# Attention's scores and products with v as 64x64 tiles, two row halves side by side, on one Trainium2 core

## The chip, the cores and the metric

The kernel runs on one core of one Trainium2 chip, in one launch. The metric is the device time of that launch in microseconds (us). A core has five engines that run their own instruction streams in order and wait for each other by semaphores: TensorE (PE, with its weight loads shown as PEld), VectorE (DVE), ScalarE (ACT), GpSimd (POOL) and SyncE (SP, which here only issues DMAs).

## The reference, cut to what matters

```
B, H, S, D = 8, 8, 576, 64; chunks of 64 tokens
scores = q_c @ k_c.T / 8                       (64x64 per batch, head and chunk)
attn   = exp(scores - max) / (sum + 1e-9)
x      = attn @ v_c  -> 4608 tokens x 512
logits = x @ w_gate                            (8 experts, 576 tokens each, by rank)
y[tokens of e] = relu(x @ w1[e]) @ w2[e]       (512 -> 1024 -> 512)
out = maximum(y @ m1, y @ m2, y @ m3) @ m_out  (512 -> 768 -> 512)
```

Everything is float32. The change touches only the first three lines of it.

## The kernel before, in words

The program has three stages: attention with the router's logits (the function `attention`), the experts, and the last layer with three weights. Only the first one changes; the second can't begin before all logits are there, so the first one's end moves what follows.

Attention works on 36 groups of 128 tokens (two chunks of 64) with all eight heads. Four groups are a unit; there are nine units, and q, k and v are loaded by units (`load_qk`, `load_v`), q and k into two buffers, v into three. One group goes through a pipeline of steps, and one pass of the loop at the end of the function (`for i in range(G + 2)`) issues one step of several groups:

- `scores(i)`: per pair of heads and per chunk one matmul. Its stationary operand is q's transpose for one chunk, [128 rows, 64 columns]: 64 rows of an even head and, under them, 64 rows of an odd head. Its moving operand is a block of `KB`, [128 rows, 128 columns], whose upper half has k's transpose of the even head in the first 64 columns and zeros in the others, and whose lower half has zeros first and then the odd head. So one matmul gives both heads' scores side by side, and half of the products are by zero.
- `trans` and `evac`: for the next unit, k and q are transposed on PE into PSUM (four transposes each) and copied to SBUF in two halves, r = 0 and 1. k's first half is copied by ACT, its second by DVE; both of q's by ACT. DVE's half of one tile waits for ACT's half.
- `smax(i)`, `ssub(i)` on DVE: maximum and subtraction, from PSUM. `expo(i)` on ACT: the exponential. `sums(i - 1)` on DVE: sum, plus 1e-9, reciprocal.
- `att_t(i - 1)`, `att_c(i - 1)`: the weights transposed on PE, copied to `AT` by ACT; `pv(i - 1)`: the product with v, again with 128 moving columns of which half are zero blocks (`VB`), into PSUM tile `pX`, which has one buffer.
- `scale(i - 2)` on DVE: `pX` times the reciprocal, and a store of x to DRAM by POOL; `x_t`, `x_c`: x transposed on PE, copied by ACT; `logit1`, `logit2`: once in four groups the gate's logits.

The zero blocks are written once, by memsets: four on DVE (first k and v buffers) and six on POOL. The order on each engine is the order in which the loop issues: there is no scheduler (`tc.manual_schedule()`). PSUM has eight banks, and all are in use: `pT` 2, `pS` 2, `pA`, `pX`, `pY`, `pL` one each.

Of the kernel before, what the change touches and what calls it, by code (L numbers as in the profile page):

```python
# [7 lines left out]
F32 = mybir.dt.float32  # L8
# [20 lines left out]
def attention(ctx, tc, q, k, v, wg_in, xd, L, ident, early, mark):  # L29
# [57 lines left out]
    def trans(nm, u, n):  # L87

        mark(nm + "T")
        if nm == "q" and n == 0:  # L90
            QT[u] = P.tile([128, 4, 8, 64], F32, name="qT")
        pt = PS.tile([128, 2, 2, 128], F32, name="pT")
        PT[nm, u, n] = pt
        for a in range(2):
            for w in range(2):
                h = 4 * (n // 2) + 2 * a + n % 2
                nc.tensor.transpose(pt[:, a, w, :], QK[nm, u][:, h, w * 128:w * 128 + 128], ident)  # L97

    def evac(nm, u, n, r, eng):
        mark(nm + "E")  # L100
        s, h0 = n % 2, 2 * (n // 2)
        src = PT[nm, u, n][r * 64:r * 64 + 64].rearrange("p a w t -> p a t w")
        o = slice(s * 64, s * 64 + 64)
        if nm == "q":
            dst = QT[u][o, h0:h0 + 2].rearrange("p a j (i w r) -> p a (j i) w r", w=2, r=2)[:, :, :, :, r]
        else:
            dst = KB[u % 2][o, :, h0:h0 + 2, s].rearrange("p j a (i w r) -> p a j i w r", w=2, r=2)[:, :, :, :, :, r]
            src = src.rearrange("p a (j i) w -> p a j i w", j=8)
        (nc.vector.tensor_copy if eng else nc.scalar.copy)(dst, src)

    def scores(g):
        mark("scores")
        u, h = divmod(g, 4)
        ps = PS.tile([128, 4, 128], F32, name="pS")
        PSS[g] = ps
        for hp in range(4):
            for c in range(2):
                nc.tensor.matmul(ps[c * 64:(c + 1) * 64, hp, :], QT[u][:, hp, 2 * h + c, :],  # L118
                                 KB[u % 2][:, 2 * h + c, hp].rearrange("p s i -> p (s i)"),
                                 start=True, stop=True)  # L120

    def smax(g):
        mark("soft")
        MX[g] = P.tile([128, 8], F32, name="mx")
        nc.vector.tensor_reduce(MX[g], PSS[g].rearrange("p a (s i) -> p (a s) i", s=2), op=OP.max, axis=AX.X)

    def ssub(g):
        mark("soft")
        A[g] = P.tile([128, 8, 64], F32, name="A0")
        nc.vector.tensor_tensor(A[g], PSS[g].rearrange("p a (s i) -> p (a s) i", s=2),  # L130
                                MX[g][:, :, None].to_broadcast([128, 8, 64]), op=OP.subtract)

    def expo(g):
# [28 lines left out]
    def pv(g):  # L162
        mark("pv")
        u, h = divmod(g, 4)
        PX[g] = PS.tile([128, 4, 128], F32, name="pX", bufs=1)
        for hp in range(4):
            for c in range(2):
                nc.tensor.matmul(PX[g][c * 64:(c + 1) * 64, hp, :], AT[g][:, hp, c * 64:c * 64 + 64],  # L168
                                 VB[u % 3][:, 2 * h + c, hp].rearrange("p s i -> p (s i)"),
                                 start=True, stop=True)  # L170

    def scale(g):
        mark("scale")
        X[g] = P.tile([128, 8, 64], F32, name="x", bufs=3)
        nc.vector.tensor_tensor(X[g], PX[g].rearrange("p a (s i) -> p (a s) i", s=2),
                                R[g][:, :, None].to_broadcast([128, 8, 64]), op=OP.mult)
        nc.gpsimd.dma_start(xd[g * 128:(g + 1) * 128, :], X[g].rearrange("p h d -> p (h d)"))

# [24 lines left out]
    def logit2(j, w0=0, w1=4):  # L203
        mark("logit2")
        pl = PS.tile([128, 4, 4, 32], F32, name="pL", bufs=1) if w0 < 3 else PS.tile([128, 4, 4, 32], F32, name="pS")
        for w in range(w0, w1):
            nc.tensor.transpose(pl[:, w].rearrange("p a e -> p (a e)"), LS[j][:, w * 128:(w + 1) * 128], ident)
        nc.vector.tensor_reduce(L[:, 4 * j + w0:4 * j + w1, :],
                                pl[:, w0:w1, :, :8].rearrange("p w a e -> p w e a"), op=OP.add, axis=AX.X)

    for n in range(4):
# [5 lines left out]
    def on(j):  # L217
        return 0 <= j < G

    for i in range(G + 2):  # L220
        u, n = i // 4 + 1, i % 4
        tr = u < NU
        if tr:
            load_v(u, n)
        if u + 1 < NU:
            load_qk(u + 1, n // 2, "kq"[n % 2])
        if on(i):
            scores(i)
        if tr:
            trans("k", u, n)  # L230
        if on(i - 1):
            att_t(i - 1)
        if tr:
            trans("q", u, n)
        if on(i - 2):
            scale(i - 2)
            if i == G + 1:
                logit1(8, 0, 3)
            x_t(i - 2)
        if on(i):  # L240
            smax(i)
        if on(i - 1):
            sums(i - 1, 0)
        if on(i):
            ssub(i)
        if on(i - 1):
            sums(i - 1, 1)
        if tr:
            evac("k", u, n, 0, 0)
        if on(i - 1):  # L250
            att_c(i - 1)
            pv(i - 1)
        if tr:
            evac("k", u, n, 1, 1)
            evac("q", u, n, 0, 0)
        if on(i):
            expo(i)
        if on(i - 1):
            sums(i - 1, 2)
        if tr:  # L260
            evac("q", u, n, 1, 0)
        if i >= 6 and (i - 3) % 4 == 3 and i < G:
            logit1((i - 3) // 4)
        if i >= 7 and (i - 4) % 4 == 3 and i < G:
            logit2((i - 4) // 4)
        if on(i - 2):
            x_c(i - 2)
        if i == G + 1:
# [932 lines left out]
```

## Time and profile before

| | before |
|---|---|
| median of 3 runs | 1247.35 us (1246.78 to 1247.45) |
| profiled execution, its own time | 1249.4 us |
| its span | 1247.6 us |
| PE busy in the span | 1190.3 us (95%), 8909 matmul records |
| DVE busy | 835.6 us (67%) |
| ACT busy | 431.9 us (35%) |
| mean granted TensorE clock | 0.982 |
| attention | from the start to about 182 us of the span |

The page of the profile shows one execution: busy time of each engine, the span in 40 slices, the DMA queues, the chain of waits that ended last, and groups of instructions by source line. The trace behind it gives every instruction's start and length, in windows or in order of time. A float32 matmul shows as two records (two passes), a transpose as one.

### The profile page before, as it was taken

The page shows a single profiled execution, that of the slowest core. Times are in us where ns is not written, and L with a number is a line of the kernel's source. Part 1 is how long each engine was busy: PE and PEld are TensorE (multiplying, and loading weights), DVE is VectorE, ACT ScalarE, POOL GpSimd, SP SyncE. Part 2 cuts the span into 40 slices and gives each one's busy share as a digit, 9 for nine tenths or more (in the row PEclk, how much of TensorE's full clock was granted, in tenths as well). Part 3 has the DMA queues.
Part 4 walks back from the last instruction along what each step waited for, and adds up shares of the span by engine and source line. Part 5 has one row for each costly group of instructions (what it writes and reads, how often), then busy time and mean ns, then how long its engine had stood idle before and what let it go on. Part 6 is the DMA issues. An engine that isn't in the chain of part 4 may idle for free.

```text
span 1247.6 us, 22277 instructions
## 1 busy us (share of the span) xinstructions
PE 1190.3 (95%) x8909; PEld 1109.0 (89%) x8909; DVE 835.6 (67%) x1686; ACT 431.9 (35%) x691; POOL 242.6 (19%) x365
## 2 busy tenths in 40 slices
PE   5999978999999999997999999999999999999996
PEld 4888854899999999997999998998998998998995
DVE  6888876887797988796824466566565565665660
ACT  3888842333334343434423122213113113113111
POOL 7222211010235344444420001001001002002001
PEclk9999996999999999999999999999999999999998
DMA  9999713364647565757653474564663663763641
GB/s 212 255 242 259 197 60 115 123 203 137 203 138 235 173 229 169 236 164 239 220 199 138 185 265 177 222 255 164 250 256 136 261 253 128 287 259 110 237 153 51
DMA packets 148778, 243.05 MB, mean 195 GB/s; under 512 B 39490, under 2 KB 111938, under 8 KB 141762
## 3 DMA queue, kind: packets, MB, share of 16 engines
q1 hardware_dynamic: 129234, 184.05, 46.2%
q0 software_dynamic: 14016, 47.98, 11.2%
q10 hardware_dynamic: 5424, 9.59, 2.1%
q8 instruction: 70, 1.15, 0.4%
q14 instruction: 34, 0.28, 0.1%
HBM read 195.12 MB, written 46.47 MB: 194 GB/s over the span
## 4 chain that ended last, share of the span: by engine, by line
PE 40%; issue 36%; DVE 13%; POOL 4%; DMA 4%; ACT 2%; POOLq 0%; SPq 0%; DVEq 0%; ACTq 0%
PE acc L1014 10%; PE acc L972 9%; PE pX L168 3%; PE pT L97 3%; PE pS L118 2%; POOL out_dram L1137 2%; PE py L1053 2%; DVE chunk L702 2%; PE po L1129 2%; DVE hlo L992 2%; DMA xg<-xd,idx 2%; PE px L1053 2%; PE pz L1053 2%; DMA inq<-in_q_dram 1%; PE pA L155 1%
## 5 line engine op out<-in xcount | busy, mean ns | idle before, releaser
L972 PE MATMUL acc<-xhi,chunk 128*128 128x288 f32 x1024 | 208.7, 303 | 8.0 <-DVE hlo L992 7.3
L1014 PE MATMUL acc<-hhi,chunk 128*128 128x288 f32 x1024 | 211.3, 300 | 2.8 <-DVE hlo L992 2.8
L972 PEld LDWEIGHTS acc<-xhi,chunk 128*128 128x128 f32 x1024 | 162.4, 190 | 9.6 <-DVE hlo L992 8.2
L1014 PEld LDWEIGHTS acc<-hhi,chunk 128*128 128x128 f32 x1024 | 162.7, 188 | 4.1 <-DVE hlo L992 3.7
L1014 PE MATMUL acc<-hlo,chunk 128*128 128x288 f32 x512 | 151.2, 295 | 1.4 <-DVE hlo L992 1.2
L1129 PE MATMUL po<-chunk,h 128*128 128x512 f32 x648 | 149.3, 390 | 0.0
L1137 POOL DMA_INDIRECT out_dram<-ot,ia x36 | 35.7, 990 | 560.6 <-ACT ot L1135 560.6
L972 PE MATMUL acc<-xlo,chunk 128*128 128x288 f32 x512 | 144.2, 297 | 0.0
L1129 PEld LDWEIGHTS po<-chunk,h 128*128 128x128 f32 x648 | 121.5, 188 | 24.8
L1053 PE MATMUL px<-xb,wa 128*128 128x384 f32 x648 | 130.0, 334 | 0.7 <-ACT ys L1021 0.7
L1053 PE MATMUL py<-xt,wb 128*128 128x384 f32 x648 | 129.8, 334 | 0.0
L1053 PEld LDWEIGHTS px<-xb,wa 128*128 128x128 f32 x648 | 114.0, 188 | 1.3 <-ACT ys L1021 1.0
L1053 PEld LDWEIGHTS py<-xt,wb 128*128 128x128 f32 x648 | 114.0, 188 | 0.5
L1074 ACT CAST h<-best 128x384 fp32r<-128x384 f32 x72 | 37.0, 513 | 198.2 <-DVE best L1072 121.3
L1014 PEld LDWEIGHTS acc<-hlo,chunk 128*128 128x128 f32 x512 | 96.0, 188 | 2.3 <-DVE hlo L992 2.3
L972 PEld LDWEIGHTS acc<-xlo,chunk 128*128 128x128 f32 x512 | 94.6, 190 | 0.0
L702 DVE TENSOR_TENSOR chunk<-raw,chunk 128x1024 fp32r<-128x1024 f32 x67 | 81.7, 1224 | 13.2 <-ACT chunk L695 13.2
L984 ACT ACTIVATE hhi<-acc 128x576 fp32r<-128x576 f32 x64 | 41.6, 650 | 110.7 <-PE acc L972 94.2
L1089 ACT COPY tmp<-px 128x384 f32<-128x384 f32 x54 | 25.8, 477 | 146.3 <-PE px L1053 146.3
L992 DVE SCALAR_TENSOR_TENSOR hlo<-acc,hhi 128x576 fp32r<-128x576 f32 x64 | 48.1, 753 | 40.5 <-ACT hhi L984 40.4
L695 ACT CAST chunk<-raw 128x1024 fp32r<-128x1024 f32 x67 | 69.7, 1047 | 9.9 <-ACT ys L1021 6.4
L732 POOL DMA_INDIRECT xg<-xd,idx x40 | 42.5, 1062 | 146.2 <-DVE ohe L622 74.9
(211 smaller groups left out, 2036.5 us busy)
## 6 DMA issues: line engine op xcount, KB each, us to landing
wb<-wdb SPq DMA_DIRECT2D x54, 1024.0 KB
wa<-wda SPq DMA_DIRECT2D x54, 768.0 KB
raw<-in_moe_w_dram SPq DMA_DIRECT2D x64, 512.0 KB
xd<-x POOLq DMA_DIRECT2D x36, 256.0 KB
yd<-ys ACTq DMA_DIRECT2D x32, 288.0 KB
wdb<-pair POOLq DMA_DIRECT2D x18, 512.0 KB
yraw<-yd SPq DMA_DIRECT2D x12, 768.0 KB
vb<-in_v_dram SPq DMA_DIRECT2D x112, 64.0 KB
```

Source lines behind the costliest of these rows:

```text
L97: nc.tensor.transpose(pt[:, a, w, :], QK[nm, u][:, h, w * 128:w * 128 + 128], ident)
L168: nc.tensor.matmul(PX[g][c * 64:(c + 1) * 64, hp, :], AT[g][:, hp, c * 64:c * 64 + 64], VB[u % 3][:, 2 * h + c, hp].rearrange("p s i -> p ...
L695: nc.scalar.copy(hi, raw)
L702: nc.vector.tensor_tensor(lo, raw, hi.bitcast(F32), op=OP.subtract)
L732: nc.gpsimd.indirect_dma_start(out=g, out_offset=None, in_=xd[:, :], in_offset=bass.IndirectOffsetOnAxis(ap=rt.idx[r][:, t:t + 1], axis=0))
L972: nc.tensor.matmul(acc[:, hf, :288], w[a][:, dc, o:o + 128], x[:, dc, tk], start=n == 0, stop=n == 11)
L984: nc.scalar.activation(hv, acc[:, :, :288], AF.Relu)
L992: nc.vector.scalar_tensor_tensor(hl[:, f].rearrange("p (a t) -> p a t", a=2), acc[:, :, :288], 0.0, hv.bitcast(F32), op0=OP.max, op1=OP.su ...
L1014: nc.tensor.matmul(acc[:, hf, :288], w[a][:, f, :], x[:, f, tk], start=n == 0, stop=n == 23)
L1053: nc.tensor.matmul(dst, w[:, dc, o, a], XO[x][:, c, dc], start=start and n == 0, stop=stop and n == 5, skip_group_check=True)
L1129: nc.tensor.matmul(PO[t], h[:, x, t % 6 * 128:t % 6 * 128 + 128], w[a][:, f % 2], start=f == 0 and n == 0, stop=f == 5 and n == 2)
L1137: st = nc.gpsimd.indirect_dma_start(out=out, out_offset=bass.IndirectOffsetOnAxis(ap=ia[:, t:t + 1], axis=0), in_=ot, in_offset=None)
```

## The change

- The zero blocks go: `VB` has [128, 8, 4, 64], k's transposes go into a tile `kT` of the same form as `qT`, and the ten memsets are gone.
- One matmul is now [64 rows, 64 columns] by 64 moving columns. There are 16 for a group's scores and 16 for its product with v, in place of 8 and 8. They are issued together by `half(g, f, e)`: in the first half the scores of group g for even heads (rows 0 to 63 of the array) beside the product of group e for odd heads (rows 64 to 127), two of the one and two of the other in turn; then `nc.tensor.drain()`; then the second half with rows swapped. Scores and product write different PSUM tiles.
- The product with v is one loop pass later: `half(i, 0, i - 2)`, and x's transposes two passes after the weights' (`x_t(i - 3)`). The loop has one pass more (G + 3).
- The order inside a pass is written anew: k's copies right behind k's transposes, `scale` ahead of `smax`, `ssub` right behind `smax`, all three steps of `sums` at the end, both of q's copies ahead of `expo`, and `x_c` last.
- x has four buffers in place of three.

```diff
                 (nc.gpsimd if u and j % 2 and s else nc.sync).dma_start(
-                    t[s * 64:(s + 1) * 64, j, :, s, :],
+                    t[s * 64:(s + 1) * 64, j],
...
-    VB = [C.tile([128, 8, 4, 2, 64], F32, name="vb%d" % i) for i in range(3)]
-    KB = [C.tile([128, 8, 4, 2, 64], F32, name="kb%d" % i) for i in range(2)]
-    for t, eng in ((KB[0], nc.vector), (VB[0], nc.vector), (KB[1], nc.gpsimd), (VB[1], nc.gpsimd),
-                   (VB[2], nc.gpsimd)):
-        eng.memset(t[0:64, :, :, 1, :], 0.0)
-        eng.memset(t[64:128, :, :, 0, :], 0.0)
+    VB = [C.tile([128, 8, 4, 64], F32, name="vb%d" % i) for i in range(3)]
...
-    def scores(g):
...
-                nc.tensor.matmul(ps[c * 64:(c + 1) * 64, hp, :], QT[u][:, hp, 2 * h + c, :],
-                                 KB[u % 2][:, 2 * h + c, hp].rearrange("p s i -> p (s i)"),
-                                 start=True, stop=True)
+    def half(g, f, e):
+
         for hp in range(4):
+            for x, s in ((g, f), (e, 1 - f)):
+                for c in range(2):
+                    o, to = slice(s * 64, s * 64 + 64), slice(c * 64, c * 64 + 64)
+                    if x == g and on(g):
+                        mark("scores")
+                        u, h = divmod(g, 4)
+                        out, a, b = PSS[g], QT["q", u][o, hp, 2 * h + c], QT["k", u][o, hp, 2 * h + c]
+                    elif x == e and on(e):
+                        mark("pv")
+                        u, h = divmod(e, 4)
+                        out, a, b = PX[e], AT[e][o, hp, to], VB[u % 3][o, 2 * h + c, hp]
+                    else:
+                        continue
+                    nc.tensor.matmul(out[to, hp, s], a, b, start=True, stop=True, tile_position=(s * 64, c * 64))
...
-    for i in range(G + 2):
+    for i in range(G + 3):
...
+        if i == G + 2:
+            logit1(8, 0, 3)
+        if on(i) or on(i - 2):
+            half(i, 0, i - 2)
+            nc.tensor.drain()
+            half(i, 1, i - 2)
         if tr:
             trans("k", u, n)
+            for r in range(2):
+                evac("k", u, n, r, r)
         if on(i - 1):
             att_t(i - 1)
-        if tr:
-            trans("q", u, n)
         if on(i - 2):
             scale(i - 2)
-            if i == G + 1:
-                logit1(8, 0, 3)
-            x_t(i - 2)
         if on(i):
             smax(i)
         if on(i - 1):
-            sums(i - 1, 0)
+            att_c(i - 1)
+        if tr:
+            trans("q", u, n)
+            for r in range(2):
+                evac("q", u, n, r, 0)
         if on(i):
             ssub(i)
...
+        if on(i - 3):
+            x_t(i - 3)
...
+            for st in range(3):
+                sums(i - 1, st)
         if on(i):
             expo(i)
...
+        if on(i - 3):
+            x_c(i - 3)
```

How the instructions stand now is shown at two places. The first is ACT in one pass in the middle of attention (`kb` or `kT`: k's half; `AT`: the transposed weights; `qT`: q's halves; `A`: the exponential; `xT`: x's transpose). Before:

```order
L109 COPY kb_178<-pT 64x2x8x32 [waits PE_49]
L160 COPY AT<-pA 128x512 [waits PE_49,Activation_49]
L109 COPY qT<-pT 64x512 [waits PE_49]
L136 ACTIVATE A<-A_1162 128x512 [waits DVE_49,Activation_49]
L109 COPY qT<-pT 64x512
L191 COPY xT<-pY 128x4x128 [waits PE_49]
```

Now:

```order
L99 COPY kT<-pT 64x512 [waits PE_49]
L157 COPY AT<-pA 128x512 [waits PE_49,Activation_49]
L99 COPY qT<-pT 64x512 [waits PE_49]
L99 COPY qT<-pT 64x512
L133 ACTIVATE A<-A_1370 128x512 [waits DVE_49,Activation_49]
L178 COPY xT<-pY 128x4x128 [waits PE_49]
```

The second copy of q has moved ahead of the exponential, which has one copy (x's) between itself and the next pass's copy of k. The second place is DVE in the same pass (`x`: the scaling, `mx` and the `A` behind it: maximum and subtraction, `sm` and `rc`: sums and reciprocal). Before:

```order
L175 TENSOR_TENSOR x<-pX,rc 128x512 [waits DMASW7_49,DVE_49,PE_49]
L125 TENSOR_REDUCE mx<-pS 128x8 [waits PE_49]
L143 TENSOR_REDUCE sm<-A 128x8 [waits Activation_49]
L130 TENSOR_TENSOR A_1300<-pS,mx 128x512 [waits DVE_49]
L145 TENSOR_SCALAR sm<-sm 128x8 [waits DVE_49]
L109 COPY kb_178<-pT 64x2x8x32 [waits Activation_49]
L148 RECIPROCAL rc<-sm 128x8 [waits DVE_49]
```

Now:

```order
L99 COPY kT<-pT 64x512 [waits Activation_49]
L162 TENSOR_TENSOR x<-pX,rc 128x512 [waits DMASW1_49,DVE_49]
L122 TENSOR_REDUCE mx<-pS 128x8
L127 TENSOR_TENSOR A_1716<-pS,mx 128x512 [waits DVE_49]
L140 TENSOR_REDUCE sm<-A 128x8
L142 TENSOR_SCALAR sm<-sm 128x8 [waits DVE_49]
L145 RECIPROCAL rc<-sm 128x8 [waits DVE_49]
```

k's copy, which waits for ACT, has moved from behind the subtraction to the head of the pass.

## Rows read from the trace of the kernel before

**Rows 1.** Windows of 10 us: busy time and records of each engine, granted clock, DMA.

```profile
core 0: us, PE busy (x) PEld busy (x) DVE busy (x) ACT busy (x) POOL busy (x), PEclk, DMA share, GB/s
...
90.00:100.00 10.00, 9.98 (x125) 9.06 (x125) 9.05 (x18) 8.35 (x16) 3.39 (x6) 1.00 1.11 242
...
130.00:140.00 10.00, 9.97 (x116) 8.21 (x115) 8.07 (x17) 8.29 (x15) 3.38 (x6) 1.00 1.15 300
...
190.00:200.00 10.00, 7.25 (x59) 3.44 (x59) 6.33 (x30) 0.00 (x0) 0.00 (x0) 0.50 0.01 2
```

**Rows 2.** Timeline of one pass, PE: start us, us, engine, line, operation, tiles.

```profile
108.39 0.66 PE L97 MATMUL pT<-ident,ink 128*128 128x128 f32 x4
...
110.29 1.11 PE L168 MATMUL pX<-vb,AT 128*64 128x128 f32 x16
...
111.21 1.06 PE L118 MATMUL pS<-kb,qT 128*64 128x128 f32 x16
...
112.20 0.66 PE L97 MATMUL pT<-ident,ink 128*128 128x128 f32 x4
```

**Rows 3.** Timeline: k's transposes of passes 3 and 31, and the stage's end.

```profile
33.96 0.33 PE L97 MATMUL pT<-ident,ink 128*128 128x128 f32 x1
...
155.98 0.66 PE L97 MATMUL pT<-ident,ink 128*128 128x128 f32 x4
...
181.98 1.20 PE L411 MATMUL rp<-ident,mm 128*128 128x128 f32 x4 [0.92 <-DVE t L392]
```

**Rows 4.** Timeline, ACT and DVE in the same passes; in brackets idle time before.

```profile
109.08 0.63 ACT L109 COPY kb<-pT 64x512 f32<-64x512 f32 x1 [0.89 <-PE pT L97]
...
109.60 0.59 ACT L160 COPY AT<-pA 128x512 f32<-128x512 f32 x1
...
110.07 0.64 ACT L109 COPY qT<-pT 64x512 f32<-64x512 f32 x1
...
110.58 0.64 ACT L136 ACTIVATE A<-A 128x512 f32<-128x512 f32 x1
...
111.24 0.64 ACT L109 COPY qT<-pT 64x512 f32<-64x512 f32 x1
...
114.30 0.70 DVE L109 COPY kb<-pT 64x512 f32<-64x512 f32 x1
...
115.03 0.20 DVE L148 RECIPROCAL rc<-sm 128x8 f32<-128x8 f32 x1
...
115.68 0.69 DVE L175 TENSOR_TENSOR x<-pX,rc 128x512 f32<-128x512 f32 x1 [0.45 <-PE pX L168]
...
116.29 0.68 DVE L125 TENSOR_REDUCE mx<-pS 128x8 f32<-128x512 f32 x1
```

**Rows 5.** Timeline of the start: k's two copies, ACT's half and DVE's half.

```profile
12.14 0.63 ACT L109 COPY kb<-pT 64x512 f32<-64x512 f32 x1 [4.84 <-PE pT L97]
...
12.80 0.69 DVE L109 COPY kb<-pT 64x512 f32<-64x512 f32 x1 [2.69 <-ACT kb L109]
```

**Rows 6.** Timeline of the last passes, without transposes of q and k.

```profile
161.98 0.68 DVE L130 TENSOR_TENSOR A<-pS,mx 128x512 f32<-128x512 f32 x1
...
162.76 0.63 ACT L136 ACTIVATE A<-A 128x512 f32<-128x512 f32 x1 [0.76 <-DVE sm L145]
...
165.33 0.68 DVE L130 TENSOR_TENSOR A<-pS,mx 128x512 f32<-128x512 f32 x1
```

**Rows 7.** The router's product, 32-column tiles: ns min/median/max, first and last start us, forms.

```profile
L600 PE MATMUL rp<-aoh x288: 179/215/249, 204.9 to 571.3; 128*32 128x40 bf16 x144
```

**Rows 8.** Timeline: one burst of that line on PE.

```profile
204.86 0.75 PE L600 MATMUL rp<-aoh 128*32 128x40 bf16 x36 [0.33 <-DVE aoh L578]
```

**Rows 9.** Timeline of the start: DVE's last memset and PE's first weight load.

```profile
8.35 1.76 DVE L79 MEMSET vb<- 64x2048 f32 x1 [0.47 <-issue]
...
10.99 0.71 PEld L97 LDWEIGHTS pT<-ident,ink 128*128 128x128 f32 x4 [10.99 <-DVE vb L79]
```

**Rows 10.** Waits of SP's queue up to 180 us: us in total, times, longest.

```profile
SPq L53 <- DMA ident<-unit: 3.8, 1, 3.8
```

More of the change, by code (lines that the diff above doesn't have):

```diff
@@ L89, in trans @@
         mark(nm + "T")
-        if nm == "q" and n == 0:
-            QT[u] = P.tile([128, 4, 8, 64], F32, name="qT")
+        if n == 0:
+            QT[nm, u] = P.tile([128, 4, 8, 64], F32, name=nm + "T")
         pt = PS.tile([128, 2, 2, 128], F32, name="pT")
@@ L102, in evac @@
         src = PT[nm, u, n][r * 64:r * 64 + 64].rearrange("p a w t -> p a t w")
[L103 to L108, printed above, removed]
-        (nc.vector.tensor_copy if eng else nc.scalar.copy)(dst, src)
-    def scores(g):
[L112 to L115, printed above, removed]
-        for hp in range(4):
-            for c in range(2):
-                nc.tensor.matmul(ps[c * 64:(c + 1) * 64, hp, :], QT[u][:, hp, 2 * h + c, :],
-                                 KB[u % 2][:, 2 * h + c, hp].rearrange("p s i -> p (s i)"),
-                                 start=True, stop=True)
+        dst = QT[nm, u][s * 64:s * 64 + 64, h0:h0 + 2].rearrange("p a j (i w r) -> p a (j i) w r", w=2, r=2)[:, :, :, :, r]
+        (nc.vector.tensor_copy if eng else nc.scalar.copy)(dst, src)
+    def half(g, f, e):
+        for hp in range(4):
+            for x, s in ((g, f), (e, 1 - f)):
[12 more added lines that the diff above has]
+                    nc.tensor.matmul(out[to, hp, s], a, b, start=True, stop=True, tile_position=(s * 64, c * 64))
     def smax(g):
@@ L124, in smax @@
         MX[g] = P.tile([128, 8], F32, name="mx")
-        nc.vector.tensor_reduce(MX[g], PSS[g].rearrange("p a (s i) -> p (a s) i", s=2), op=OP.max, axis=AX.X)
+        nc.vector.tensor_reduce(MX[g], PSS[g].rearrange("p a s i -> p (a s) i"), op=OP.max, axis=AX.X)
     def ssub(g):
@@ L160, in att_c @@
         nc.scalar.copy(AT[g], PA[g])
[L162 to L170, printed above, removed]
     def scale(g):
         mark("scale")
-        X[g] = P.tile([128, 8, 64], F32, name="x", bufs=3)
-        nc.vector.tensor_tensor(X[g], PX[g].rearrange("p a (s i) -> p (a s) i", s=2),
+        X[g] = P.tile([128, 8, 64], F32, name="x", bufs=4)
+        nc.vector.tensor_tensor(X[g], PX[g].rearrange("p a s i -> p (a s) i"),
                                 R[g][:, :, None].to_broadcast([128, 8, 64]), op=OP.mult)
@@ L209, in logit2, with on @@
                                 pl[:, w0:w1, :, :8].rearrange("p w a e -> p w e a"), op=OP.add, axis=AX.X)
+    def on(j):
+        return 0 <= j < G
     for n in range(4):
@@ L227, in attention @@
         if on(i):
-            scores(i)
+            PSS[i] = PS.tile([128, 4, 2, 64], F32, name="pS")
+        if on(i - 2):
+            PX[i - 2] = PS.tile([128, 4, 2, 64], F32, name="pX", bufs=1)
+        if i == G + 2:
[4 more added lines that the diff above has]
+            half(i, 1, i - 2)
         if tr:
             trans("k", u, n)
+            for r in range(2):
+                evac("k", u, n, r, r)
         if on(i - 1):
             att_t(i - 1)
-        if tr:
-            trans("q", u, n)
         if on(i - 2):
             scale(i - 2)
-            if i == G + 1:
-                logit1(8, 0, 3)
-            x_t(i - 2)
         if on(i):
@@ L242, in attention @@
         if on(i - 1):
-            sums(i - 1, 0)
+            att_c(i - 1)
[3 more added lines that the diff above has]
+                evac("q", u, n, r, 0)
         if on(i):
             ssub(i)
-        if on(i - 1):
[L247 to L255, printed above, removed]
+        if on(i - 3):
+            x_t(i - 3)
+        if i >= 7 and i % 4 == 3 and i < G:
+            logit1((i - 7) // 4)
+        if i >= 8 and i % 4 == 0 and i < G + 1:
+            logit2((i - 8) // 4)
+        if on(i - 1):
+            for st in range(3):
+                sums(i - 1, st)
         if on(i):
             expo(i)
[L258 to L268, printed above, removed]
+        if on(i - 3):
+            x_c(i - 3)
+        if i == G + 2:
             early()
```

4 lines of the change are left out of this document (1 added, 3 removed).

## Prediction

> **What bounds the kernel now.** I read the windows first. From 30 to 150 us attention is in a steady state, and in the stretch from 90 to 100 us PE is busy for 9.98 of 10 us at the full granted clock, DVE for 9.05, ACT for 8.35, while the DMA engines show a share of 1.11 at 242 GB/s [rows 1]. Three engines and the DMAs are all close to full, so shortening one of them is worth no more than the next one leaves. Then the timeline, for one pass of the loop. On PE k's transposes start at 108.39, the product with v at 110.29, the scores at 111.21, the next pass's transposes at 112.20 [rows 2]: 1.90 us of transposes and 1.91 us of the two products that the change touches, with no gap worth naming. PE sets the pace here. The mean pass, with the gate's logits in one of four and some stalls, is longer: from pass 3 to pass 31 the transposes move from 33.96 to 155.98 us [rows 3], 122.0 us for 28 passes, **4.36 us a pass**. The stage ends with the router's first matmul at 181.98 us [rows 3]. The sum below is made against this execution's own time of 1249.4 us, which is 2.05 us over the median of 1247.35.
>
> **What the change does to PE.** The two products take 1.11 and 1.06 us for 16 records each, overlapping a little [rows 2]: two column tiles at a time with 128 moving columns. Now there are 64 records a pass in two halves of 32, with 64 moving columns. No operation of this form is in the trace, so I bound it. From below: four tiles at once, the same array time in half as many steps; two halves at a quarter of the columns each would be about 0.5 us for both products plus what each half needs to finish. From above: still only two tiles at a time, so 32 records of 64 columns take what 16 of 128 take, 1.1 us a half, 2.2 us, plus the drain and the change of form. The nearest row is the router's product in 32-column tiles, where 36 records take 0.75 us with their end [rows 8]: 32 of them 0.67 us, two halves 1.33, and 0.2 for drain and change of form. I take **1.5 us** (bounds 0.9 and 2.4) in place of 1.91. PE alone would then need 1.90 + 1.5 = 3.4 us a pass.
>
> **What it does to the chain between ACT and DVE.** This is the term that I think decides. The order shows two moves: k's copy by DVE now stands at the head of DVE's pass, ahead of scaling, maximum and subtraction, and on ACT nothing is left behind the exponential but x's copy before the next pass's copy of k. DVE's copy of k waits for ACT's copy of the other half: at the start of the run ACT's begins at 12.14 and takes 0.63, DVE's begins at 12.80 having waited for ACT [rows 5], 0.66 later. So each pass closes a ring, all on instructions that wait for the one before:
>
> - ACT's copy of k until DVE's copy of k starts: 0.66 [rows 5].
> - DVE's copy until the scaling starts: 0.73 by the pair copy, reciprocal (114.30 to 115.03), 0.61 by the pair scaling, maximum (115.68 to 116.29) [rows 4]. No row has this pair; I take 0.67.
> - Scaling to maximum 0.61 [rows 4]; the maximum 0.68 [rows 4] with about 0.03 until the dependent subtraction starts, as between the two copies, 0.71.
> - Subtraction until the exponential starts, where ACT is idle: 161.98 to 162.76, 0.78 [rows 6].
> - Exponential until the next ACT instruction: 110.58 to 111.24, 0.66 [rows 4].
> - x's copy until the next pass's copy of k: 0.47, as from one PSUM copy to the next, 109.60 to 110.07 [rows 4].
>
> The sum is **4.56 us a pass**, and I take it. Lower bound: 0.61 for the copy and 0.68 + 0.03 for the subtraction, 4.43. Upper: 0.73 for the copy, 0.69 for the scaling, and x's copy at its full 0.59, 4.82. Before, no such ring closed in one pass, since DVE copied k behind the subtraction. So PE's 3.4 us is not what a pass takes. The ring through PE is shorter too: transposes to ACT's copy 0.69 (108.39 to 109.08), 0.66, 0.67 and 0.69 of scaling [rows 4, 5], which frees `pX` for the product, then 1.5: 4.21 us. It would bind from products of 1.85 us on. The product's wait for `pX` is new on PE; behind it stand the same pass's transposes of k, for which ACT waits, and this is in the ring. The loads don't bind: a pass moves four times 0.262 MB, which at the 242 to 300 GB/s of the windows [rows 1] is 4.33 to 3.5 us, under 4.56. SP's queue keeps its order; on POOL x's store waits for the scaling as before, one store and one load of v a pass, with four buffers of x in place of three: 0.
>
> **The sum.** 28 passes at 4.56 - 4.36 = 0.20: **+5.6 us** (bounds +2.0 and +12.9). First three passes: k's copies, 0.66 + 0.73, now come ahead of the first maximum, and the first weights are transposed that much later; part of it lies beside transposes: **+0.5** (0 to +1.4). The last passes, without q and k: DVE's own 0.61 + 0.71 + 0.61 + 0.6 and 0.4 of small ones are 2.9 us where a pass took 165.33 - 161.98 = 3.35 [rows 6], four passes, -1.8; against it x's transposes of group 34 now come behind the last product, and the logits wait for them and their copy, 0.44 + 0.69 + 0.59 = +1.7 [rows 4]. **0** (-1.8 to +1.7). The memsets: DVE's last ends at 10.11 us, but PE's first weight load starts at 10.99 [rows 9], when SP too gets on after 3.8 us of waiting for the identity [rows 10], so the identity's load is the cover and the memsets cost nothing; without that cover they would be worth 0.9. POOL's six end late, and its first three loads of v, 0.19 MB, go about 11 us earlier, into a stretch where the next unit's q and k are loaded: 0 (to +0.8). v's pieces stay 256 bytes long in DRAM: 0. The extra pass holds no step that wasn't on the last group's path. Sum: +6.1 us, so 1255.5 for the profiled execution and **1253.5 us** for the median. What follows attention is unchanged and moves with it.
>
> **A page that speaks against the change.** The Trainium skill (TensorEngine Tiling (Array Packing), Instruction Overhead) says that each matmul has some 60 cycles of overhead, and that one shouldn't take a tiling factor from a dimension that is already small, which 64 columns are. At the full clock that is an estimate of 25 ns a record. In the rows 36 records take 0.75 us, of which the last one's length is 0.215 [rows 7, 8]: (0.75 - 0.215)/35 = 15 ns apart, less than the page says, with four column tiles; no row has two row halves. By the page's figure two halves would take an estimated 2 x (0.8 + 0.215) + 0.2 = 2.2 us, between the two prices of the second rival below.
>
> **The rivals.** A measurement of this kernel can tell about 0.2%, 2.5 us, from no change.
>
> *The ring is as tight as its tightest pairs* (4.43 us), and the start costs nothing: +2.0 us, 1249.3 us, no change that can be told. For it: the scaling and maximum, two instructions on PSUM like the copy and the scaling, start 0.61 apart [rows 4]. Against: the pair that begins with the copy itself.
>
> *The products are slow.* Small matmuls could queue one behind another instead of running four at a time. Before, 16 records of 128 columns take 1.1 us, 69 ns apart [rows 2]; at half of that for half the columns two halves take 2.2 us, with 0.2 for drain and change of form 2.4. The ring through PE decides from 1.85 us on; at 2.4 a pass takes 2.71 + 2.4 = 5.11, 28 x 0.75 + 0.5 = +21.5, 1268.9 us, and midway, at 2.1, +13.1 and 1260.5 us, which I take as its price. For it: each of the 64 records loads its own weights, and two row halves side by side are in no row. Against: rows 8.
>
> *Faster: the ring does not close.* If DVE's copy of k need not wait for ACT's in the steady state, the pass is PE's or the loads': PE's 3.4 us, and the loads at between 3.5 and 4.33. At 4.1, 28 x -0.26 + 0.5 = -6.8: 1240.6 us. It decides once a pass comes under 4.36. For it: 0.41 us of PE's time really goes, and PE is the engine that is full. Against: the order names a wait for ACT at DVE's copy in every pass, and the start shows what it waits for [rows 5].
>
> *The clock falls.* PE would be busy for 3.4 of 4.56 us, 75%; from 190 to 200 us it was busy for 7.25 of 10 and granted 0.50 [rows 1]. At that level transposes and products would take near 6.5 us a pass (twice 3.4, less what overlaps): 28 x 2.1 = +59, 1306 us. Against: there the work is a chain of single small matmuls, here it comes in bursts of over 1 us.
>
> That the change doesn't do what it says is no rival: the order has 64x64 matmuls in twos and twos.
>
> **How the numbers follow.** The forecast has 0.52, the tight ring 0.18, slow products 0.13, the open ring 0.12, the clock 0.05. The range 1246.0 to 1266.0 holds the forecast's own bounds (1249.9 to 1260.7 with the start's term), the tight ring, and slow products up to 2.3 us; it leaves out the open ring and the clock, 0.17, and the top of the slow products. Slower by over 0.2%: forecast, slow products and clock, 0.70. Within 0.2%: the tight ring, 0.18. Faster: 0.12.
>
> **What would show it.** In the trace after: passes near 4.56 us; PE idle for about 1 us a pass ahead of the product, released by DVE's scaling; ACT idle ahead of the exponential, released by DVE, and DVE idle ahead of k's copy, released by ACT; a burst of products with drain of 1.5 us; the stage's end at about 188.1 us; loads that land earlier ahead of their use; the stretches after attention as long as before. I'm wrong if DVE's copy of k starts without having waited for ACT, if a pass is under 4.4 us, if PE is busy throughout, or if the granted clock in attention is not 1.00.

## The result, and the profile after

| | before | after |
|---|---|---|
| median of the runs | 1247.40 us (1246.78 to 1249.42, 4 runs) | 1265.55 us (1263.13 to 1267.33, 4 runs) |
| ratio | | 1.0141, 95% interval 1.0120 to 1.0163 |
| profiled execution, its span | 1247.6 us | 1265.5 us |

The change makes the kernel 18.1 us slower, where 6.1 was forecast: 1265.55 us, not 1253.5. The stage first, on PE: k's transposes of passes 3 and 31 and the stage's end, as in [rows 3].

```profile
33.08 0.66 PE L92 MATMUL pT<-ident,ink 128*128 128x128 f32 x4
...
171.43 0.66 PE L92 MATMUL pT<-ident,ink 128*128 128x128 f32 x4
...
198.24 0.98 PE L397 MATMUL rp<-ident,mm 128*128 128x128 f32 x3 [0.91 <-DVE t L378]
```

The 28 passes take 138.35 us, 4.94 each, in place of 122.02 and 4.36: +16.3 us. Start and tail together are 59.9 us against 60.0. What follows attention takes 1067.3 us against 1065.6; in the experiments below it takes 1064 to 1070 in every run that has all the loads, so that part is the spread of single executions. (The three runs that leave loads out compute other numbers in attention and take 1061 to 1063 behind it, so their totals overstate what attention gains by some 2 to 5 us.)

The pass was forecast by a ring of ACT and DVE. ACT in four passes (the exponential of each shows the period):

```profile
105.72 0.63 ACT L133 ACTIVATE A<-A 128x512 f32<-128x512 f32 x1 [1.24 <-DVE A L127]
106.38 0.59 ACT L178 COPY xT<-pY 128x512 f32<-128x512 f32 x1
106.99 0.62 ACT L99 COPY kT<-pT 64x512 f32<-64x512 f32 x1
...
110.48 0.63 ACT L133 ACTIVATE A<-A 128x512 f32<-128x512 f32 x1 [0.99 <-DVE A L127]
111.13 0.59 ACT L178 COPY xT<-pY 128x512 f32<-128x512 f32 x1
111.62 0.62 ACT L99 COPY kT<-pT 64x512 f32<-64x512 f32 x1
...
115.10 0.63 ACT L133 ACTIVATE A<-A 128x512 f32<-128x512 f32 x1 [1.25 <-DVE A L127]
...
119.86 0.63 ACT L133 ACTIVATE A<-A 128x512 f32<-128x512 f32 x1 [0.35 <-DVE A L127]
...
124.36 0.63 ACT L133 ACTIVATE A<-A 128x512 f32<-128x512 f32 x1 [1.25 <-DVE A L127]
```

And DVE in the second of them:

```profile
107.65 0.69 DVE L99 COPY kT<-pT 64x512 f32<-64x512 f32 x1 [0.78 <-ACT kT L99]
108.37 0.69 DVE L162 TENSOR_TENSOR x<-pX,rc 128x512 f32<-128x512 f32 x1
108.98 0.68 DVE L122 TENSOR_REDUCE mx<-pS 128x8 f32<-128x512 f32 x1
109.69 0.69 DVE L127 TENSOR_TENSOR A<-pS,mx 128x512 f32<-128x512 f32 x1
```

Follow it round: ACT's copy of k 106.99, DVE's 107.65, scaling 108.37, maximum 108.98, subtraction 109.69, exponential 110.48, x's copy 111.13, the next copy of k 111.62. Nothing in it waits for anything outside it, and where an engine has been idle its bracket names the other one. Four passes take 124.36 - 105.72 = 18.64 us, **4.66 a pass**. That explains 28 x 4.66 - 122.02 = 8.5 of the 16.3 us. The rest is in passes that are not regular. Windows of 10 us:

```profile
60.00:70.00 10.00, 7.32 (x120) 6.62 (x121) 5.23 (x12) 5.05 (x9) 1.75 (x3) 0.66 1.02 243
70.00:80.00 10.00, 7.83 (x164) 5.79 (x163) 7.28 (x14) 7.40 (x13) 2.34 (x4) 1.00 1.19 222
...
90.00:100.00 10.00, 7.11 (x97) 5.41 (x94) 6.30 (x12) 5.67 (x10) 2.19 (x4) 0.83 0.74 179
100.00:110.00 10.00, 8.38 (x201) 7.11 (x197) 7.11 (x16) 7.48 (x13) 1.97 (x5) 1.00 1.09 243
```

From 60 to 70 and from 90 to 100 us PE, DVE and ACT are all less busy than in the windows beside them, and the granted clock falls to 0.66 and 0.83. The waits from 28 to 180 us (us in total, times, longest) give the ring and the rest:

```profile
DVE kT L99 <- ACT kT L99: 32.9, 30, 3.7
ACT A L133 <- DVE A L127: 28.2, 31, 1.5
...
PE pX L117 <- DVE x L162: 8.9, 13, 1.0
...
PE pS L117 <- issue: 4.0, 3, 2.6
...
PE pX L117 <- issue: 3.6, 4, 1.9
...
PE pT L92 <- issue: 1.1, 1, 1.1
...
PE pA L152 <- issue: 1.0, 1, 1.0
```

"issue" is idle time for which the profile names no releaser. The timeline of PE has five such gaps of 0.9 us and more:

```profile
39.37 0.44 PE L152 MATMUL pA<-ident,A 128*128 128x128 f32 x2 [0.98 <-issue]
...
62.55 0.37 PE L117 MATMUL pS<-kT,qT 64*64 64x64 f32 x2 [2.62 <-issue]
...
79.13 0.21 PE L117 MATMUL pS<-kT,qT 64*64 64x64 f32 x1 [1.24 <-issue]
...
86.69 0.33 PE L92 MATMUL pT<-ident,inq 128*128 128x128 f32 x1 [1.09 <-issue]
...
95.06 0.21 PE L117 MATMUL pX<-vb,AT 64*64 64x64 f32 x1 [1.91 <-issue]
```

They come in the middle of anything, even between two records of one product. What is late is found in the packets of the DMA engines. In the stretch of the longest gap, 59.93 to 62.55 us, the queues show one packet of instructions on q8 among the loads (and one of 8192 bytes on another instruction queue, q14):

```profile
q1 hardware_dynamic: 921, 0.51, 97.3%
q0 software_dynamic: 42, 0.11, 13.8%
q8 instruction: 1, 0.02, 2.6%
```

Counted over the trace, q8 brings 16384 bytes each time, once in about 255 records of PE (weight loads, matmuls, drains and waits, in order of start). These are PE's instructions: up to the end of attention q8 brings 24 packets here and 15 in the kernel before, as PE's records go from 3860 to 6150, while q14 brings 12 and 13. Below, a block is 256 records, what one such packet brings. Numbering the records gives, for the five gaps:

```
gap ends   PE idle   record   rest by 256   after the end of q8's last packet
  39.37     0.98       705       193          1.77
  62.55     2.62      1473       193          1.53
  79.13     1.24      1985       193          1.99
  86.69     1.09      2241       193          1.68
  95.06     1.91      2497       193          1.50
```

So PE has run out of instructions at the end of a block, and goes on 1.5 to 2.0 us after the next block's packet. That packet ended on average 4.6 us after PE had begun the block ahead of it (longest 7.3, from 40 to 140 us), and a block lasts about 7.6 us. The kept traces of all 17 kernels bear this out: with the blocks counted from remainder 193, no block begins sooner than 1.2 us after its packet has ended. The shortest distance is 1.2 to 1.4 us in each of the nine traces with the tiles and the loads, and 1.66 us and more in the eight others. The clock was granted at its lower level (1.2 GHz) from 61.6 us, inside the longest gap, to 68.4, and from 95.7 to 99.1, behind the second longest; behind the three others it stayed at 2.4 GHz.

### The profile page after: what moved, and what is told of

Read it like the earlier page. It is cut to its first block, busy times and chain, and to the rows that moved or that the text cites. A ratio compares the mean times of both kernels' runs of the same rounds, so it can differ in the third digit from the quotient of the medians.

```text
span 1265.5 us, 24559 instructions
## 1 busy us (share of the span) xinstructions
PE 1178.9 (93%) x10061; PEld 1095.3 (87%) x10061; DVE 834.0 (66%) x1682; ACT 431.3 (34%) x691; POOL 231.3 (18%) x359
## 4 chain that ended last, share of the span: by engine, by line
issue 36%; PE 29%; DVE 20%; ACT 5%; POOL 4%; DMA 4%; POOLq 0%; SPq 0%; ACTq 0%; DVEq 0%
PE acc L1000 8%; PE acc L958 8%; DVE chunk L688 2%; POOL out_dram L1123 2%; PE py L1039 2%; DMA xg<-xd,idx 2%; DVE hlo L978 2%; PE po L1115 2%; DVE kT L99 2%; PE px L1039 2%; DVE A L127 1%; ACT kT L99 1%; PE pz L1039 1%; DVE x L162 1%; DVE mx L122 1%
```

## The experiments

My theory: the ring makes 8.5 us, and PE waiting for its own instructions, which come behind the loads, makes the rest, with the clock. The rivals: the loads pace the passes, the small products are slow, or the stalls belong to the row halves and the drain.

**The ring and the loads: four runs.** *late* moves one copy and opens the ring:

```diff
             trans("k", u, n)
-            for r in range(2):
-                evac("k", u, n, r, r)
+            evac("k", u, n, 0, 0)
...
             ssub(i)
+        if tr:
+            evac("k", u, n, 1, 1)
```

> One move in the changed kernel: DVE's copy of k from the head of its pass to behind the subtraction. Theory of the ring and the stalls: the ring of 4.66 us a pass no longer closes, and the regular passes fall to 4.1 to 4.35 us, where PE, DVE and the loads are all near full; the stalls of PE in which the trace names no one it waits for (some 8 us in three or four passes of the changed kernel) stay or get worse. Attention ends at 182 to 193 us, the time is 1247 to 1258 us. Theory that the loads set the pace: regular passes stay at 4.6 us or more, 1262 to 1268 us. Theory that the products of 64x64 are slow on PE: the same, with PE's burst of products longer than 1.85 us.

*few* leaves out the loads of q and k from the third unit on and those of v for three units, so that old contents are used again; *late_few* has both edits:

```diff
+            if u > 1:
+                QK[nm, u] = QK[nm, u - 2]
+                continue
...
+        if 2 < u < 6:
+            return
```

> The changed kernel without the loads of q and k from the third unit on, and without those of v for units 3 to 5 (old contents are used again). Theory of the ring and the stalls: the regular passes stay within 0.05 of 4.66 us, since the ring has no load in it; the stalls of PE without a named releaser are gone in passes 8 to 20, and the granted clock stays at 1.00 there, since PE's instructions come through the same DMA engines as the loads and those are now nearly idle. Attention ends at 188 to 192 us, the time is 1254 to 1259 us. Theory that the loads set the pace: the passes fall under 4.4 us, 1249 us or less. Theory that the stalls are PE's own (too many instructions to fetch, whatever the loads do): they stay, 1262 to 1267 us.

> Both edits together: DVE's copy of k behind the subtraction, and the loads left out. Theory of the ring and the stalls: with the ring open and the loads gone, the pass is set by DVE or PE, 3.6 to 4.1 us; attention ends at 166 to 178 us, the time is 1232 to 1245 us. If passes stay at 4.2 us or more, neither the ring nor the loads bound the pass, and PE or DVE does at a price that I have wrong.

*oldprod* has the new order and the old products:

```diff
-            half(i, 0, i - 2)
-            nc.tensor.drain()
-            half(i, 1, i - 2)
+        if on(i):
+            scores(i)
+        if on(i - 2):
+            pv(i - 2)
```

> The new order of the loop with the old products: 128 rows and 128 moving columns with the zero blocks and their memsets, product with v one pass later, as in the changed kernel. Theory of the ring and the stalls: the ring closes as in the changed kernel and the regular passes are 4.6 to 4.8 us, but PE has 64 records fewer a pass to fetch and stalls less: attention ends at 189 to 194 us, the time is 1254 to 1260 us. Theory that the small products cost the time: the passes are back at 4.36 us, 1246 to 1250 us. If it stays at 1262 us or more, the stalls don't come from the number of PE's instructions.

| run | median us | against before, 95% | pass, us | gaps without releaser, 0.9 us and more |
|---|---|---|---|---|
| late | 1244.07 | 0.9954 to 0.9991 | 4.15 (mean of 28, stalls included) | 2 |
| few | 1254.99 | 1.0037 to 1.0060 | 4.66 (regular) | 0 |
| late_few | 1232.95 | 0.9848 to 0.9900 | 4.02 (mean of 28) | 0 |
| oldprod | 1259.80 | 1.0074 to 1.0109 | 4.72 (regular) | 0 |

The means are taken from exponential to exponential.

One moved copy brings the kernel from 18.1 us above the one before to 4.1 us below it, faster than I had expected (1247 to 1258 us). Of this 28 x (4.66 - 4.15) = 14.3 us are the passes against the ring's; the rest is that the changed kernel's stalls come on top of its 4.66, while those of *late* are in its 4.15. DVE in the pass of *late* that I read has no gap left, and k's copy waits for no one:

```profile
117.70 0.69 DVE L162 TENSOR_TENSOR x<-pX,rc 128x512 f32<-128x512 f32 x1
118.31 0.68 DVE L122 TENSOR_REDUCE mx<-pS 128x8 f32<-128x512 f32 x1
119.03 0.69 DVE L127 TENSOR_TENSOR A<-pS,mx 128x512 f32<-128x512 f32 x1
119.75 0.70 DVE L99 COPY kT<-pT 64x512 f32<-64x512 f32 x1
```

Without the loads the ring's passes are the same to 0.01 us, and the stalls and the low clock are gone: the 28 passes of *few* take 130.4 us, 4.66 each in the mean, where the changed kernel's take 138.35. Windows of *few*, and under them *oldprod*, which has all the loads but half as many records of products.

```profile
60.00:70.00 10.00, 8.43 (x171) 6.79 (x169) 8.05 (x17) 7.60 (x14) 1.10 (x2) 1.00 0.13 54
90.00:100.00 10.00, 9.34 (x205) 7.24 (x204) 8.03 (x17) 7.63 (x14) 1.11 (x3) 1.00 0.34 101
```

```profile
60.00:70.00 10.00, 9.45 (x117) 7.89 (x115) 8.06 (x17) 7.20 (x13) 2.69 (x5) 1.00 1.14 237
90.00:100.00 10.00, 9.77 (x111) 7.62 (x110) 7.75 (x17) 8.11 (x15) 2.35 (x4) 1.00 1.12 231
```

The order alone, then, costs 11.6 us (*oldprod* against the runs of before beside it, 1248.16), and the tiles the rest, each time against the runs of before beside it: 6.5 of the 18.1 us, or 3.5 of the 15.1 us that the changed kernel showed when it was run again (*after2*, below). The loads don't pace the ring.

**The ring's length, twice more.** *longer* puts one instruction into it, *xearly* takes one out:

```diff
+        if on(i - 1):
+            sums(i - 1, 0)
         if on(i):
             ssub(i)
```

> The changed kernel with the sum over the weights (DVE, 0.68 us) moved from behind the subtraction to ahead of it: one more instruction in the ring. Theory of the ring: the regular passes grow by that instruction's 0.70 us from 4.66 to 5.35, 28 passes +19.6 us, less some 4 to 6 us of stalls, since PE's instructions are spread over more time: 1278 to 1285 us. Theory that PE or the loads set the pace: DVE's work is the same in sum, so 1263 to 1268 us.

```diff
+        if on(i - 3):
+            x_c(i - 3)
         if on(i):
             expo(i)
-        if on(i - 3):
-            x_c(i - 3)
```

> The changed kernel with x's copy on ACT moved from behind the exponential to ahead of it, where ACT has been idle for 1.0 to 1.25 us: one instruction less in the ring, and k's copy on DVE left at the head. Theory of the ring: the regular passes lose 0.49 to 0.61 us, from 4.66 to 4.1 to 4.25 us, if PE has k's transposes ready by then; stalls as in the run with the copy of k moved; 1244 to 1254 us. Theory that DVE's place for k's copy itself is what matters: 1262 to 1267 us.

*longer*: 1273.77 us (1.0175 to 1.0222), passes of 5.13. The ring grew, so neither PE nor the loads set the pace, but by 0.47 us and not 0.70, and the time stayed under the range that I gave. DVE there:

```profile
107.88 0.68 DVE L122 TENSOR_REDUCE mx<-pS 128x8 f32<-128x512 f32 x1
108.48 0.68 DVE L140 TENSOR_REDUCE sm<-A 128x8 f32<-128x512 f32 x1
109.07 0.68 DVE L127 TENSOR_TENSOR A<-pS,mx 128x512 f32<-128x512 f32 x1
```

The three start 0.60 and 0.59 apart, and none needs the one just before it; maximum and subtraction side by side, where the second needs the first, start 0.71 apart. So the instruction costs 0.60 + 0.59 - 0.71 = 0.48.

*xearly*: 1259.72 us (1.0071 to 1.0105), above what the theory of the ring gave and under what its rival gave. The regular passes fell to 4.33, not 4.1 to 4.25, so the ring did get shorter; but the mean of the 28 is 4.62, with two gaps of 1.07 and 1.90 us without a releaser and shorter ones. The next ring is the one through PE, and ACT now waits for it at k's copy:

```profile
115.77 0.62 ACT L99 COPY kT<-pT 64x512 f32<-64x512 f32 x1 [0.28 <-PE pT L92]
```

From DVE's scaling (117.15) to the product it releases (117.98) 0.83, to k's transposes (119.57) 1.59, to ACT's copy of k 0.69, to DVE's 0.68, to the scaling 0.73: 4.52 in this pass. I had this ring at 4.21, with 0.69 in place of 0.83 and 1.5 in place of 1.59.

**What the tiles bring.** *late_old* is *oldprod* with the copy of k moved as in *late*; *late_old_few* leaves the loads out as well.

> The new order with DVE's copy of k behind the subtraction (the ring open), and the old products with their zero blocks and memsets. It tells what the small tiles bring once the ring is open, beside the run that has both. Theory of the ring and the stalls: regular passes of 4.1 to 4.4 us with PE busy for over 95%, no stall without a named releaser, since PE's instructions come every 10 to 12 us as in the kernel before; 1244 to 1250 us, so that the tiles bring some 3 us or nothing, their shorter passes being eaten by stalls. If it is 1241 us or less, the tiles themselves cost time even with the ring open.

> The open ring with the old products, and the loads left out as before. It tells what the tiles bring where nothing holds up PE's instructions, beside the run with tiles, the open ring and no loads (1233 us). Theory that PE paces the old products and DVE the tiles: regular passes of 4.2 to 4.3 us against 3.98, 28 passes some 6 to 9 us, 1237 to 1242 us. If it comes out at 1235 us or less, the tiles bring nothing even there.

1243.34 us (0.9936 to 0.9969), just under the range that I gave, and 1238.62 (0.9892 to 0.9947), both with passes of 4.25 in the mean and no such gap. PE is busy without a break in this window of *late_old*:

```profile
60.00:70.00 10.00, 10.00 (x123) 8.21 (x122) 9.42 (x18) 9.38 (x17) 3.32 (x6) 1.00 1.13 255
```

So with the ring open the tiles are worth 0.23 us a pass where no loads are in the way (4.02), 5.7 us in all; with the loads 0.1 us a pass or less (4.15, and 4.19 in *late2*), and the times of *late* and *late_old* can't be told apart. The traces with tiles have two and four stalls and the one with the old products none, so what the tiles save seems to go into stalls. *late* once more (*late2*) gave 1243.73 us (0.9947 to 0.9974), with four such gaps. With the ring open, then, the kernel beats both the changed kernel and the one before, the latter by 0.3 to 0.5%, with either kind of product.

> The kernel with DVE's copy of k moved behind the subtraction, once more, beside the three below on one chip. It should come out as before: 1241 to 1247 us, with two to four stalls of PE without a releaser, each beginning when PE has gone through a whole number of blocks of 256 records since the last such stall, and ending 1.2 to 2.0 us after the packet that brought a block.

**What makes a block late.** *split* is *oldprod* with each product cut in two, *late_split* the same with the ring open:

```diff
-                nc.tensor.matmul(ps[c * 64:(c + 1) * 64, hp, :], QT[u][:, hp, 2 * h + c, :],
-                                 KB[u % 2][:, 2 * h + c, hp].rearrange("p s i -> p (s i)"),
+                for s in range(2):
+                    nc.tensor.matmul(ps[c * 64:(c + 1) * 64, hp, s * 64:s * 64 + 64], QT[u][:, hp, 2 * h + c, :],
+                                     KB[u % 2][:, 2 * h + c, hp, s], start=True, stop=True)
```

> The new order with the old products, each of them cut into two of 64 moving columns: as many PE records a pass as the changed kernel has (64 for the products in place of 32), no row halves, no drain, the ring closed. Theory that the stalls are PE waiting for its own instructions behind the loads: a block of PE's instructions comes every 7 to 8 us again, in place of 10 to 12, and stalls of 1 us and more without a releaser come back, each ending 1.4 to 1.7 us after such a block's packet; 1262 to 1268 us. Theory that the stalls belong to the row halves, the swap or the drain: none, regular passes of 4.7 us throughout, 1258 to 1261 us.

> The open ring with the old products, each cut into two of 64 moving columns: as many PE records as with the tiles, no row halves and no drain. The passes are PE's, some 4.3 to 4.6 us, so a block of 256 records takes 6 to 7 us as with the tiles and the open ring. Theory that any kernel whose blocks are this short stalls behind the loads: two to four stalls at remainder 193. Theory that only the small tiles' program is hit (as the run with split products and the closed ring had none): no stalls. The time by PE: 1244 to 1254 us without stalls, some 3 to 5 us more with them.

*spread* puts k's transposes between the halves:

```diff
             half(i, 0, i - 2)
-            nc.tensor.drain()
-            half(i, 1, i - 2)
         if tr:
             trans("k", u, n)
...
+            nc.tensor.drain()
+            half(i, 1, i - 2)
```

> The open ring with k's transposes put between the two halves of the products, so that 64 records come in one burst in place of 128; as many records a pass as before. Theory that a stall comes wherever a block of PE's instructions takes longer to arrive than PE takes for a block (6.0 to 6.5 us): stalls as in the run beside it, 1241 to 1248 us. Theory that it is the length of a burst: no stalls, 1237 to 1241 us.

*late_vb* and *after_ms* give v the old layout, the second with the old number of memsets, and *after2* is the changed kernel again:

> The same with v's pieces written 512 bytes apart in SBUF (as in the kernel before, without zeros) in place of 256 bytes apart. In the traces so far a block of PE's instructions came 3.2 to 3.4 us after PE began the block ahead of it in three kernels with v laid out that way, 4.2 to 5.0 us in four with the small tiles' layout, though 5.3 us in the kernel before. Theory that v's layout sets this delay: 3.5 us or less, no stalls, 1237 to 1241 us. Theory that it is chance or something else: 4 us or more, stalls as in the run beside it, 1241 to 1247 us.

> The changed kernel with as many memsets on DVE and POOL as the kernel before had, over a v tile of the old form of which only half is used: v's first loads on POOL go out late again, as in the kernels with the old products, which had no stalls. Theory that the earlier loads of v set the phase of loads against PE's blocks: no stalls, 1256 to 1260 us. Theory that the memsets don't matter: 1262 to 1268 us.

> The changed kernel once more, to see whether its stalls recur. 1263 to 1268 us; four or five stalls, each at a record whose number leaves the remainder 193 when divided by 256, as in its first trace; if the same few numbers recur (705, 1473, 1985, 2241, 2497), something fixed in the program makes those blocks late; if they move from run to run, the delay is chance in the queues.

| run | median us | against before, 95% | gaps | a block lasts (mean, us) | its packet ends after the block ahead began (mean, longest) |
|---|---|---|---|---|---|
| split | 1260.48 | 1.0080 to 1.0113 | 0 | 7.2 | 3.2, 5.9 |
| late_split | 1246.17 | 0.9964 to 0.9992 | 0 | 6.6 | 3.3, 4.6 |
| spread | 1252.60 | 1.0015 to 1.0047 | 2 | 6.8 | 4.5, 6.5 |
| late_vb | 1243.07 | 0.9944 to 0.9975 | 2 | 6.4 | 4.6, 7.6 |
| after_ms | 1264.74 | 1.0104 to 1.0146 | 2 | 7.5 | 5.0, 7.8 |
| after2 | 1264.82 | 1.0086 to 1.0141 | 2 | 7.6 | 5.1, 8.2 |

Of the nine kernels with the tiles and the loads only *longer* has no such gap. In the other eight traces there are 21, and all stand at remainder 193. (For one of the two of *spread*, 1.41 us, the profile names DVE's sums, which the transposes behind the gap don't need; it stands at remainder 193 too and ends 1.5 us after its packet.) *after2* showed two gaps where I had expected four or five, but the same records recur: 1985 and 2497 in all three traces of the changed kernel's order. So which blocks can be late seems to be fixed by where they end in the pass; how late they are changes from trace to trace, and the time may vary with it (1261.2 to 1270.5 for *after2*).

*split* and *late_split* have as many records and as short blocks, and no stall. So my account by the number of records and the loads alone falls. What came true, times included, is the rival's forecast: that the stalls belong to the tiles' program, with its row halves, swap and drain. If their blocks too end at remainder 193, where no stall shows it, a block's packet comes 1 to 2 us sooner after PE began the one ahead than in the tiles' kernels, and no block begins sooner than 1.66 us after its packet. That isn't the loads: these add about as much for the old products (*late_old* 3.4 us against 0.6 in *late_old_few*) as for the tiles (4.7 in *late* against 2.4 in *late_few*). Nor do packets come late with the tiles only: in the kernel before they end 5.3 us after PE began the block ahead, but there a block lasts 10.5 us. So a stall takes short blocks, the loads, and something in the tiles' program by which the block is asked for late or needed early. Neither v's layout nor the memsets are it, and *spread* shows that a burst of half the length doesn't end the stalls. What it is stays open: no run has the tiles without the drain or without the swap of row halves, and none has the split products without the loads. *spread* came out above both its ranges, and lost its time to something else: PE waits for k's copy by DVE, and ACT waits longer for the transposed weights (waits, 28 to 165 us; in *late* from 28 to 160 us each of the two is 1.2 us in all):

```profile
ACT AT L157 <- PE pA L152: 23.1, 31, 3.0
...
PE pT L92 <- DVE kT L99: 6.8, 11, 0.8
```

## Why the prediction was wrong in size

- **The ring: right in mechanism, low in size.** All seven steps are there, in the order foretold, and 4.66 us stands against 4.56. Copy of k to scaling takes 0.72 where I took 0.67, between its bounds; x's copy to k's takes 0.49 and 0.61 in turn where I took 0.47 from one pair, which is most of the 0.10. 28 passes gave +8.5 us in place of +5.6, within the bounds of +2.0 to +12.9.
- **The step that failed** is the sum's silence on PE between the passes: it put 28 equal passes of 4.56 us and no term for stalls, and gave no reason for leaving it out; of what came, its list of what would prove it wrong has only the clock. The irregular passes cost 16.3 - 8.5 = 7.8 us, and without the loads, in *few*, 7.9 us are gone. They hold five gaps of PE, 7.8 us together by chance: the ring hides part of them, and the stretches at the lower clock add to them. In these gaps PE waits for its next block of instructions. Put at nothing, this term is larger than the error of the ring, 2.9 us. There was a reason to ask for it: the DMAs had a share over 1 [rows 1], and the change gives PE 64 records more a pass. But *split*, with both, has no stall, so these two would not have given its size, and why the tiles' blocks come too late stays open.
- **The products: right.** After the scaling's start at 103.62 the first product goes at 104.45, k's transposes at 105.87: 1.42 us against 1.5, and 1.39 to 1.44 in most other passes. No row gave the 0.2 in it for the drain and the change of form; from the last start of one half (104.92, in the group at 104.82) to the first of the other it is 0.32.

```profile
103.62 0.69 DVE L162 TENSOR_TENSOR x<-pX,rc 128x512 f32<-128x512 f32 x1
...
104.45 0.27 PE L117 MATMUL pX<-vb,AT 64*64 64x64 f32 x2 [0.25 <-DVE x L162]
104.47 0.27 PE L117 MATMUL pS<-kT,qT 64*64 64x64 f32 x2
104.53 0.25 PE L117 MATMUL pX<-vb,AT 64*64 64x64 f32 x2
104.57 0.23 PE L117 MATMUL pS<-kT,qT 64*64 64x64 f32 x2
104.59 0.25 PE L117 MATMUL pX<-vb,AT 64*64 64x64 f32 x2
104.63 0.22 PE L117 MATMUL pS<-kT,qT 64*64 64x64 f32 x2
...
104.82 0.31 PE L117 MATMUL pX<-vb,AT 64*64 64x64 f32 x4
105.24 0.27 PE L117 MATMUL pS<-kT,qT 64*64 64x64 f32 x2
...
105.87 0.66 PE L92 MATMUL pT<-ident,ink 128*128 128x128 f32 x4
```

  From 104.53 on four records start every 0.06 us, 15 ns each, as in [rows 8]. By the Trainium skill (TensorEngine Tiling (Array Packing), Instruction Overhead) it would be 25 ns at the full clock, as an estimate from its 60 cycles a matmul; the trace does not agree. The rival of slow products falls.
- **The open ring** fell for the changed kernel. *late* shows what it would have given: 1244 us for a rival put at 1240.6.
- **The clock** fell, but not by the road of that rival: *few* keeps 1.00 all through attention, with PE busy for 7.70 to 9.45 of 10 us in its windows. In the changed kernel it fell inside a gap of 2.62 us and behind one of 1.91.
- **What would show it:** DVE's and ACT's brackets came as foretold; PE is idle ahead of the product, released by the scaling, in only 13 passes, 8.9 us, not about 1 us in every one (its first scores go ahead). The stage ends at 198.24 us, not 188.1.
- **Start and tail** together came to -0.1 us against +0.5. No cost of the memsets shows, as forecast: *after_ms* has as many of them back, and its interval lies on the changed kernel's.

For the blocks, the Trainium skill (Runtime: NRT & Kernel Launch, Instruction fetch mechanics) says that an engine's instructions come in blocks of 16 KiB, 256 instructions, the next one fetched while the present one runs. The packets of 16384 bytes and the one remainder, 193, agree. It also says that the cost of crossing a block is mostly hidden; here it was for the old products, whole or cut in two, and PE stood for up to 2.62 us at such a place with the tiles.

## What to carry to other kernels

When a change writes a new order, walk round every chain that two engines close within a pass, and price each pair by rows of that pair, dependent or not: here one copy, put ahead of three instructions that did not need it, was worth some 22 us, stalls included. Work that leaves PE comes back only where PE set the pace, and what takes its place should be looked for next. A gap that the profile puts down to no one need not be noise: number the engine's records, and see whether the gaps stand at a fixed remainder and behind an instruction packet.

## What the runs showed of the hardware that I had not expected

- PE's instructions share the DMA engines with the loads. With the loads on, a block's packet ended 4.7 us after PE began the block ahead (*late*), without them 2.4 (*late_few*); with the old products 3.4 (*late_old*) and 0.6 (*late_old_few*). With the tiles, stalls of up to 1.6 us came with this at blocks of 6.4 us (*late*), of up to 2.62 us at 7.6 us (the changed kernel). No block in any trace began sooner than 1.2 us after its packet.
- Two DVE instructions on 128x512 start 0.60 us apart, but 0.71 when the second needs the first. Pairs with k's copy (64x512) are another matter: the scaling doesn't need the copy, and yet starts 0.72 behind it (107.65 to 108.37).
- Matmuls of 64x64 in two row halves start as tightly as four column tiles, 15 ns a record; between the halves, with the drain, the last start of one and the first of the next lie 0.32 us apart (104.92 to 105.24).
